# Batch 1's queries loaded ahead of the weights, softmax work spread over two slots, and a third output buffer, in a fused linear attention and highway layer

## The chip, the cores and the metric

The kernel runs on one core of a Trainium2 chip. The core has four compute engines that run beside each other, each through its own list of instructions in order: PE (matrix multiplies, into the accumulator memory PSUM), DVE (vector work), ACT (activations and copies) and POOL (vector work that can't reach PSUM). SP only starts transfers (DMAs) between main memory and on-chip memory. The metric is device time in microseconds (us), and the number compared is the median of repeated runs.

## The reference

The inputs are q, k and v of shape 8 x 8 x 576 x 64 (batch, head, sequence, head dimension), two weight matrices of 512 x 512 and a bias of 512. Attention without the square score matrix comes first: queries are softmaxed over the head dimension, keys over the sequence, and each head needs only a 64 x 64 product of keys and values. A highway layer follows.

```python
q_s = exp(q - max(q, -1));  q_s = q_s / (sum(q_s, -1) + 1e-09)
k_s = exp(k - max(k, 2));   k_s = k_s / (sum(k_s, 2) + 1e-09)
kv  = einsum('bhsd,bhse->bhde', k_s, v)
x   = einsum('bhsd,bhde->bhse', q_s, kv)      # then 4608 tokens x 512
H = maximum(x @ w_h, 0.0)
T = 1.0 / (1.0 + exp(-(x @ w_t + b_t)))
out = T * H + (1.0 - T) * x
```

## The kernel before

**Attention of one batch.** Each of the 8 batches has its q, k and v loaded as float32 tiles of 128 partitions x 2304, 1.18 MB each (`load`, L92). ACT takes the exponential of q and k in two halves each (`exp_half`, L154: 128 x 1152 to fp16). DVE sums the exponentials of q over the head dimension (`q_sums`, L199) and takes the reciprocal. The scaling of q by it has three forms: on DVE with an fp16 copy of the reciprocals (`q_scale_v`, L206 to L212, batches 0 and 2), by halves on POOL and DVE (`q_scale_half`, L217 to L227, batch 1), and on POOL (`q_scale_p`, L236, batches 3 to 7). PE transposes the scaled queries (`q_trans`, tile pq) and DVE copies them out (qsT, L253). POOL casts v to fp16 (`cast_v`, L161), PE multiplies keys and values (`kv_half`, tile psk), and DVE normalises the product (`kv_norm`, L186 and L188, tile kvn). PE multiplies queries by it (`x_pair` and `x_left`, tiles px and px_l). ACT copies three of the four px tiles into xT (L275), and DVE the fourth (L277) and the two small leftovers (L290, tile x9, which collects the last 64 rows of every batch).

**Highway layer of one batch.** The layer runs on transposed x, in four blocks of 128 output columns. `gate(c, ob)` is four matmuls (tile pt, 128 x 512) and a tanh on ACT (L308); `carry(c, ob)` is four matmuls (tile ph) and one DVE instruction for max(H, 0) - x (tile dd, L317); `blend(c, ob)` is one DVE instruction that multiplies the two (tile g, L325). `out_tile` turns x and g back by matmuls with identities (tile nat), copies them to an output buffer (ACT, L356, and in the last group also DVE, L354) and after every fourth tile starts a DMA of 1 MB (L359). Index c = 8 stands for the leftover rows; `most9` and `last9` write them.

**What sets the order.** Nothing is scheduled by a tool: each engine executes its instructions in the order in which the code emits them. A first list (L452 to L468) is emitted, then a table of events by half steps p. Slot c is the eight steps from p = 8c to 8c + 7, with the highway layer of batch c; the attention work of batch c + 1 is placed in the same slot, and part of the softmax of the next. Waits follow from data and from buffers. PSUM has eight banks: four for pt and ph in turn (`ps_ht`), three for pq, psk and px in turn (`ps_q`) and one for nat. Since the four `ps_ht` banks go round, gate or carry number n waits until DVE has finished with number n - 4.

**Transfers.** All loads and stores are started by SP in one order: q, k and v of batch 0 in halves, the bias, w_t, w_h, then q, k, v of batch 1, and so on; stores stand between the loads of later batches. The load tiles rotate over three buffers for each of q, k and v, and the weights use one turn of the q and the k tiles. The weights are cast to fp16 by DVE (w16t and one block of w16h) and POOL (three blocks of w16h). The output buffer o32 has two turns; the leftover rows have a buffer of their own (o9). In the last group, the second output buffer of group 3 is the one that group 2's second DMA reads.

Of the kernel before, what the change touches and what calls it, by code (L numbers as in the profile page):

```python
# [9 lines left out]
FP32 = mybir.dt.float32  # L10
FP16 = mybir.dt.float16
# [7 lines left out]
def kernel(  # L19
# [180 lines left out]

    NG = [(0, 4), (4, 8), (8, 9)]

    def q_scale_v(b):
        r32 = qsum[b]
        r2 = small.tile([P, 4 * N9, 2], FP16, tag="r2", name=f"r2_{b}")
        nc.vector.reciprocal(r32, r32)  # L206
        flat = r32.rearrange("p n c -> p (n c)")
        nc.vector.tensor_copy(r2, flat.broadcast_to([P, 4 * N9, 2]))
        e = eq[b].rearrange("p n c (w t) -> p (n c) w t", t=2)
        rb = r2.unsqueeze(2).broadcast_to([P, 4 * N9, 32, 2])  # L210
        for s in (slice(0, 16), slice(16, 4 * N9)):
            nc.vector.tensor_mul(e[:, s], e[:, s], rb[:, s])  # L212

    def q_scale_half(b, a, eng):
        h = slice(2 * a, 2 * a + 2)
        r32 = qsum[b][:, :, h]
        nc.vector.reciprocal(r32, r32)  # L217
        if eng is nc.gpsimd:
            e = eq[b][:, :, h, :]
            eng.tensor_mul(e, e, r32.broadcast_to(list(e.shape)))  # L220
            return
        r2 = small.tile([P, N9, 2, 2], FP16, tag="r2h", bufs=1, name=f"r2_{b}_{a}")
        nc.vector.tensor_copy(r2, r32.broadcast_to([P, N9, 2, 2]))
        e = eq[b][:, :, h, :].rearrange("p n c (w t) -> p n c w t", t=2)
        for c in range(2):
            rb = r2[:, :, c].unsqueeze(2).broadcast_to([P, N9, 32, 2])
            nc.vector.tensor_mul(e[:, :, c], e[:, :, c], rb)  # L227

    def q_recip(b):
        nc.vector.reciprocal(qsum[b], qsum[b])  # L230

    def q_scale_p(b, i):
        s = (slice(0, 4), slice(4, N9))[i]
        e = eq[b][:, s]
        r = qsum[b][:, s]
        nc.gpsimd.tensor_mul(e, e, r.broadcast_to(list(e.shape)))  # L236

    def q_trans(b, g, eng=None):
# [142 lines left out]
    def last9():  # L381
        t = ps_ht.tile([P, 4, P], FP32, tag="ht", name="nat9_l")
# [9 lines left out]
    def at(p, *fs):  # L392
        events.setdefault(p, []).extend(fs)

    E = lambda f, *a: (lambda: f(*a))

    for c in range(B + 1):
# [4 lines left out]
    for c in range(B + 1):  # L402
        for ob in range(4):
            at(8 * c + 2 * ob + 2, E(blend, c, ob))

# [7 lines left out]
                at(p + 1 + i // 2, E(out_tile, g, i, True))  # L413
    at(8 * B + 8, E(most9), E(last9))

    at(0, E(exp_half, 1, "q", 1))
    at(1, E(q_sums, 1, 0), E(q_scale_half, 1, 0, nc.gpsimd))
    at(3, E(q_sums, 1, 1), E(q_scale_half, 1, 1, nc.vector))
    at(5, E(exp_half, 1, "k", 0), E(cast_v, 1, 0))
    at(6, E(exp_half, 1, "k", 1), E(cast_v, 1, 1))  # L420
    at(7, E(q_trans, 1, 0), E(q_trans, 1, 1, nc.scalar), E(q_trans, 1, 2))
    at(7, E(kv_half, 1, 0), E(kv_half, 1, 1), E(kv_norm, 1))
    at(7, E(x_pair, 1, 0), E(x_pair, 1, 1), E(x_left, 1))
    for b in range(2, B):
        p = 8 * (b - 1)
        s = p + {2: 0, 3: -4}.get(b, -5)
        at(s, E(exp_half, b, "q", 0))
        at(s + 1, E(exp_half, b, "q", 1), E(q_sums, b, 0))
        at(s + 2, E(q_sums, b, 1))
        if b == 2:  # L430
            at(s + 2, E(q_scale_v, b))
        else:
            at(s + 2, E(q_recip, b), E(q_scale_p, b, 0))
            at(s + 3, E(q_scale_p, b, 1))
        s = p + {2: 2, 3: 0}.get(b, -1)
        at(s, E(exp_half, b, "k", 0), E(cast_v, b, 0))
# [12 lines left out]
    for b in range(2, B):  # L449
        at(8 * max(b - 3, 0), *[E(load, b, w) for w in "qkv"])  # L450

    for f in [  # L452
        E(warm_up, 20),
        E(exp_half, 0, "q", 0), E(q_sums, 0, 0),
        E(exp_half, 0, "q", 1), E(q_sums, 0, 1),
        E(q_scale_v, 0),
        E(exp_half, 0, "k", 0), E(cast_v, 0, 0),
        E(exp_half, 0, "k", 1), E(cast_v, 0, 1),
        E(q_trans, 0, 0), E(q_trans, 0, 1), E(warm_up, 2), E(q_trans, 0, 2),
        E(warm_up, 6),  # L460
        E(kv_half, 0, 0), E(gate_bias), E(warm_up, 2), E(kv_half, 0, 1), E(kv_norm, 0),
        E(warm_up, 4),
        E(x_pair, 0, 0), E(warm_up, 2), E(x_pair, 0, 1), E(warm_up, 2), E(x_left, 0),
        E(warm_up, 2),
        *[E(cast_weight, "t", k_, nc.vector) for k_ in range(4)],
        *[E(cast_weight, "h", k_, (nc.gpsimd, nc.vector)[k_ // 3]) for k_ in range(4)],
        E(exp_half, 1, "q", 0),
    ]:  # L468
        f()
    for p in range(8 * (B + 1) + 1):  # L470
        for f in events.pop(p, []):
            f()
    assert not events, events
# [30 lines left out]
```

## Time and profile before

| | |
|---|---|
| median of 13 runs | 148.41 us |
| lowest to highest | 146.84 to 151.21 us |
| the profiled execution's own time | 148.12 us |
| its span in the trace | 146.2 us |
| PE, DVE, ACT, POOL busy | 122.8, 108.2, 88.0, 43.9 us |

The difference between the profiled execution's time and its span, 1.9 us, lies around the span. The profile gives for each group of instructions the busy time, the mean duration and the idle time of the engine just before it, with what ended that idle time. The chain of waits is followed back from the last instruction to what released it. A view by windows gives the busy time of each engine in any stretch, with PEclk, the clock that TensorE was granted (1.00 is full speed), and what the DMA engines moved. A timeline lists instructions in order of time with the idle time in front of them. Several instructions on one timeline row overlap a little, so the distance between starts is what one costs its engine.

### The profile page before, as it was taken

The numbers are of one execution on the slowest core, as the hardware profiler recorded it, in microseconds if no ns is written. First come the engines' busy times: TensorE is split into PE (matmuls) and PEld (weight loads), VectorE is DVE, ScalarE is ACT, GpSimd is POOL, SyncE is SP. The second block draws the span as 40 slices with busy tenths as digits, with TensorE's granted clock in tenths as the row PEclk, the third lists the DMA queues.
The fourth block names the chain that finished last, engine by engine and source line by source line (L and its number), as shares of the span: only waits on it lengthen the run. The fifth ranks groups of instructions, "written<-read, shape, count | busy, mean of one in ns | idle before, by whom it ended". The sixth has DMA issues, their size and how long they took to land.

```text
span 146.2 us, 3509 instructions
## 1 busy us (share of the span) xinstructions
PE 122.8 (84%) x1465; PEld 66.6 (46%) x1465; DVE 108.2 (74%) x201; ACT 88.0 (60%) x125; POOL 43.9 (30%) x38
## 2 busy tenths in 40 slices
PE   4979968355908968997999899899989999999940
PEld 1345323143405422663664475466447555577530
DVE  1493579993698696699679988987998666574860
ACT  3660409724683546769869778796973664552630
POOL 2006042901400019605920890393098000000000
PEclk9999999999996895999999999999999999999997
DMA  4999999999999999500399999993006006037466
GB/s 161 345 400 390 401 404 411 411 412 415 402 410 411 412 404 412 206 2 0 135 276 409 404 313 364 402 395 119 0 4 287 9 0 287 0 141 318 191 263 239
DMA packets 16023, 40.06 MB, mean 274 GB/s; under 512 B 644, under 2 KB 1672, under 8 KB 14984
## 3 DMA queue, kind: packets, MB, share of 16 engines
q1 hardware_dynamic: 16008, 39.85, 71.1%
q8 instruction: 11, 0.18, 0.5%
q14 instruction: 4, 0.03, 0.1%
HBM read 30.41 MB, written 9.44 MB: 273 GB/s over the span
## 4 chain that ended last, share of the span: by engine, by line
PE 50%; DVE 33%; DMA 7%; ACT 4%; issue 2%; SPq 0%; DVEq 0%; ACTq 0%
PE pt L59 15%; PE ph L59 14%; DVE r L199 11%; PE nat L59 6%; PE pq L64 5%; DVE g L325 5%; DVE dd L317 5%; PE psk L59 5%; DMA out_dram<-o 4%; DMA q<-in_q_dram 3%; PE warm L59 3%; PE px L59 2%; DVE xT L277 2%; ACT eq L154 2%; DVE w16t L111 1%
## 5 line engine op out<-in xcount | busy, mean ns | idle before, releaser
L308 ACT ACTIVATE pt<-pt,bt 128x512 f32<-128x512 f32 x36 | 23.8, 663 | 27.4 <-PE pt L59 27.4
L59 PE MATMUL pt<-xT,w16t 128*128 128x512 f16 x128 | 35.5, 393 | 3.7 <-DVE xT L277 2.6
L59 PE MATMUL ph<-xT,w16h 128*128 128x512 f16 x128 | 34.3, 392 | 3.7 <-DVE g L325 3.7
L236 POOL TENSOR_TENSOR eq<-eq,r 128x1024 f16<-128x1024 f16 (+1 forms) x10 | 21.0, 2117 | 42.5 <-DVE r L230 42.5
L317 DVE SCALAR_TENSOR_TENSOR dd<-ph,xT 128x512 f16<-128x512 f32 x32 | 21.9, 686 | 10.8 <-PE ph L59 10.8
L325 DVE SCALAR_TENSOR_TENSOR g<-pt,dd 128x512 f16<-128x512 f32 x36 | 24.4, 678 | 1.4
L199 DVE TENSOR_REDUCE r<-eq 128x18 f32<-128x1152 f16 x16 | 21.5, 1345 | 4.0 <-ACT eq L154 3.9
L161 POOL CAST v<-v 128x1152 f16<-128x1152 f32 x16 | 18.2, 1162 | 17.0 <-DMA v<-in_v_dram 10.1
L154 ACT ACTIVATE eq<-q 128x1152 f16<-128x1152 f32 x16 | 18.4, 1163 | 6.7 <-DMA q<-in_q_dram 6.7
L59 PEld LDWEIGHTS <-w16h 128*128 128x128 f16 x144 | 12.7, 100 | 18.1 <-issue 8.5
L59 PEld LDWEIGHTS <-w16t 128*128 128x128 f16 x144 | 12.8, 99 | 16.1 <-DVE w16t L111 2.5
L154 ACT ACTIVATE ek<-k 128x1152 f16<-128x1152 f32 x16 | 18.5, 1169 | 1.6 <-DMA k<-in_k_dram 1.6
L59 PE MATMUL nat<-half_i,g 128*128 128x128 f16 x140 | 18.9, 219 | 0.2 <-DVE g L325 0.2
L356 ACT COPY o<-nat 128x512 f32<-128x512 f32 x28 | 16.5, 591 | 3.4 <-PE nat L59 2.8
L275 ACT CAST xT<-px 128x512 f16<-128x512 f32 x24 | 13.4, 592 | 8.2 <-PE px L59 8.0
L59 PE MATMUL nat<-ident,xT 128*128 128x128 f16 x128 | 17.3, 219 | 0.0
L64 PE MATMUL pq<-ident,eq 128*128 128x128 f16 x144 | 12.1, 224 | 4.7 <-DVE eq L212 4.7
L59 PEld LDWEIGHTS <-g 128*128 128x128 f16 x144 | 14.0, 98 | 4.1 <-DVE g L325 0.6
L253 DVE COPY qsT<-pq 128x1024 f16<-128x1024 f16 (+1 forms) x23 | 12.4, 548 | 4.3 <-PE pq L64 4.2
L59 PEld LDWEIGHTS <-xT 128*128 128x128 f16 x128 | 12.5, 98 | 5.2 <-issue 2.4
L59 PE MATMUL warm<-wide,ident 128*128 128x512 f16 x40 | 12.8, 464 | 1.9 <-DVE wide L140 1.9
L64 PEld LDWEIGHTS <-eq 128*128 128x128 f16 x144 | 9.7, 100 | 8.3 <-ACT ek L154 5.6
(48 smaller groups left out, 88.7 us busy)
## 6 DMA issues: line engine op xcount, KB each, us to landing
out_dram<-o SPq DMA_DIRECT2D x8, 1024.0 KB, 4.7
q<-in_q_dram SPq DMA_DIRECT2D x7, 1152.0 KB, 14.4
k<-in_k_dram SPq DMA_DIRECT2D x7, 1152.0 KB, 14.5
v<-in_v_dram SPq DMA_DIRECT2D x6, 1152.0 KB, 14.6
v<-in_v_dram SPq DMA_DIRECT2D x4, 576.0 KB, 11.0
q<-in_q_dram SPq DMA_DIRECT2D x2, 576.0 KB, 4.1
k<-in_k_dram SPq DMA_DIRECT2D x2, 576.0 KB, 7.1
w32t<-in_moe_w_t_dram SPq DMA_DIRECT2D x1, 1024.0 KB, 11.1
```

The lines of the kernel that those rows point to most:

```text
L59: mm = lambda o, l, r, st, sp: nc.tensor.matmul(o, l, r, start=st, stop=sp, skip_group_check=True)
L64: nc.tensor.matmul(o, i, ident, is_transpose=True, start=True, stop=True, skip_group_check=True,)
L154: nc.scalar.activation(dst[b][:, :, 2 * a : 2 * a + 2, :], in32[which][b][:, 2 * a : 2 * a + 2].rearrange("p c n d -> p n c d"), AF.Exp,)
L161: (eng or nc.gpsimd).tensor_copy(v16s[b % 2][:, :, 2 * a : 2 * a + 2, 0:64], in32["v"][b][:, 2 * a : 2 * a + 2].rearrange("p c n d -> p n ...
L199: nc.vector.reduce_sum(qsum[b][:, :, h], eq[b][:, :, h, :], axis=AX.X)
L236: nc.gpsimd.tensor_mul(e, e, r.broadcast_to(list(e.shape)))
L253: nc.vector.tensor_copy(qsT[b][:, :, n0:n1, :], t[:, :, 0:w, :])
L275: nc.scalar.copy(dst, t[c])
L308: nc.scalar.activation(ps, ps, AF.Tanh, bias=bt2[:, ob : ob + 1], scale=0.5)
L317: nc.vector.scalar_tensor_tensor(dd, ps, 0.0, xv(ob), op0=ALU.max, op1=ALU.subtract)
L325: nc.vector.scalar_tensor_tensor(gv(ob), th, 1.0, dd, op0=ALU.add, op1=ALU.mult)
L356: nc.scalar.copy(o, flat(t))
```

## The change

- The load of batch 1's queries is put ahead of the two weights on SP. Nothing else changes place on that queue.
- Slot 0 is no longer built from the table: its instructions are written out in the first list. Batch 1's exponentials stand on ACT directly behind batch 0's last copies, and its sums and scaling stand on DVE on both sides of the cast of w_t and ahead of all of slot 0's dd and g. It is scaled on DVE only. Two blocks of w16h are cast by ACT and two by POOL, none by DVE. Twelve more warm-up matmuls (tile warm) stand ahead of the first gate. Gates 0 and 1 stand ahead of carries 0 and 1, and batch 1's transposes and products stand between the later gates and carries.
- Batch 2's query exponentials and its first sum move from slot 1 to the end of slot 0. Its scaling moves from DVE to POOL (`q_scale_p`), the second half of its v cast moves from POOL to DVE, and its two products of keys and values stand one step earlier, its transposes one or no step later.
- Batch 3's query exponentials and sums move from the middle of slot 1 to its last two steps and the first step of slot 2; its scaling follows in slot 2, behind both of its v casts. Batch 4's query softmax moves from p = 19 to 22 to p = 20 to 23, and batch 4 takes the plan that batch 3 had.
- `q_scale_v` works on row groups 0 to 3 and 4 to 8 with an fp16 copy of the reciprocals for each, which is one small cast more (batches 0 and 1); `q_scale_half` is gone.
- The pool `og` has three buffers instead of two, and the leftover rows' buffer o9 becomes one turn of it.

On DVE in slot 0, from the weight cast on, before. The names are the tiles of the sections above with their shapes; r_1 are batch 1's sums, eq batch 1's queries, pt_0 and ph_0 the first block of batch 0's highway layer.

```order
L111 CAST w16t<-w32t 128x512 x4
L111 CAST w16h<-w32h 128x512
L317 SCALAR_TENSOR_TENSOR dd_0_369<-ph_0_364,xT_299 128x512
L199 TENSOR_REDUCE r_1_371<-eq_342 128x9x2
L217 RECIPROCAL r_1_371<-r_1_371 128x9x2
L325 SCALAR_TENSOR_TENSOR g_344<-pt_0_345,dd_0_369 128x8x64
L317 SCALAR_TENSOR_TENSOR dd_1_387<-ph_1_382,xT_299 128x512
L199 TENSOR_REDUCE r_1_371<-eq_342 128x9x2
L217 RECIPROCAL r_1_371<-r_1_371 128x9x2
L223 CAST r_1_1_391<-r_1_371 128x36
L227 TENSOR_TENSOR eq_342<-eq_342,r_1_1_391 128x9x64 x2
L325 SCALAR_TENSOR_TENSOR g_344<-pt_1_375,dd_1_387 128x8x64
```

The same place now.

```order
L199 TENSOR_REDUCE r_1_350<-eq_347 128x9x2
L111 CAST w16t<-w32t 128x512 x4
L199 TENSOR_REDUCE r_1_350<-eq_347 128x9x2
L204 RECIPROCAL r_1_350<-r_1_350 128x36
L210 CAST r_1_0_358<-r_1_350 128x32
L212 TENSOR_TENSOR eq_347<-eq_347,r_1_0_358 128x1024
L210 CAST r_1_4_361<-r_1_350 128x40
L212 TENSOR_TENSOR eq_347<-eq_347,r_1_4_361 128x1280
L297 SCALAR_TENSOR_TENSOR dd_0_389<-ph_0_384,xT_300 128x512
L305 SCALAR_TENSOR_TENSOR g_368<-pt_0_369,dd_0_389 128x8x64
```

Both sums and the whole scaling of batch 1 have moved in front of the first dd and g, and the w16h cast has left DVE.

On DVE at the end of slot 1 and the start of slot 2, before: kvn is batch 2's normalised product, r_3 are batch 3's sums, px_1_1 is batch 2's fourth product (it goes into xT), and g_344 with pt_2 and pt_3 are the last two blocks of slot 1.

```order
L188 TENSOR_TENSOR kvn_103<-psk_1_639,rz_725 128x128
L199 TENSOR_REDUCE r_3_731<-eq_676 128x9x2
L325 SCALAR_TENSOR_TENSOR g_344<-pt_2_621,dd_2_683 128x8x64
L199 TENSOR_REDUCE r_3_731<-eq_676 128x9x2
L230 RECIPROCAL r_3_731<-r_3_731 128x36
L317 SCALAR_TENSOR_TENSOR dd_3_757<-ph_3_752,xT_299 128x512
L277 CAST xT_740<-px_1_1_760 128x8x64
L290 CAST x_107<-px_l_767 128x2x64
L290 CAST x_107<-px_l_773 128x2x64
L325 SCALAR_TENSOR_TENSOR g_344<-pt_3_733,dd_3_757 128x8x64
```

The same place now.

```order
L188 TENSOR_TENSOR kvn_103<-psk_1_622,rz_713 128x128
L297 SCALAR_TENSOR_TENSOR dd_2_723<-ph_2_718,xT_300 128x512
L233 COPY qsT_666<-pq_1_725 128x4x256
L233 COPY qsT_666<-pq_2_735 128x4x64
L305 SCALAR_TENSOR_TENSOR g_368<-pt_2_659,dd_2_723 128x8x64
L297 SCALAR_TENSOR_TENSOR dd_3_762<-ph_3_757,xT_300 128x512
L257 CAST xT_746<-px_1_1_765 128x8x64
L270 CAST x_107<-px_l_772 128x2x64
L270 CAST x_107<-px_l_778 128x2x64
L199 TENSOR_REDUCE r_3_785<-eq_755 128x9x2
L305 SCALAR_TENSOR_TENSOR g_368<-pt_3_739,dd_3_762 128x8x64
L199 TENSOR_REDUCE r_3_785<-eq_755 128x9x2
```

Batch 3's sums stood in front of the cast of px_1_1 and now stand behind it.

The core of the diff:

```diff
-    og = pool("og", 2)
+    og = pool("og", 3)
...
     nc.sync.dma_start(brow, moe_b_t.rearrange("(k p) -> k p", p=P))
+    load(1, "q")
     load_weight("t", moe_w_t, "q32")
     load_weight("h", moe_w_h, "k32")
-    load(1, "q")
...
+    def q_scale_v(b, n0, n1):
+        w = 4 * (n1 - n0)
+        r2 = small.tile([P, w, 2], FP16, tag=f"r2_{w}", name=f"r2_{b}_{n0}")
+        r = qsum[b][:, n0:n1].rearrange("p n c -> p (n c)")
+        nc.vector.tensor_copy(r2, r.broadcast_to([P, w, 2]))
+        e = eq[b][:, n0:n1].rearrange("p n c (w t) -> p (n c) w t", t=2)
+        nc.vector.tensor_mul(e, e, r2.unsqueeze(2).broadcast_to([P, w, 32, 2]))
...
+        o9 = o32["last"] = og.tile([P, 4, 512], FP32, tag="o32", name="o9")
...
+    at(8, E(q_sums, 2, 1), E(q_recip, 2), E(cast_v, 2, 0), E(q_scale_p, 2, 0, 4))
+    at(9, E(exp_half, 2, "k", 0), E(q_scale_p, 2, 4, N9))
+    at(10, E(exp_half, 2, "k", 1))
+    at(11, E(cast_v, 2, 1, nc.vector))
...
+            s = p + {3: -2, 4: -4}.get(b, -5)
...
+            2: ((4, 5, 5), (3, 4), (6, 7, 7)),
+            3: ((4, 5, 5), (3, 4), (6, 7, 7)),
+            4: ((2, 3, 4), (4, 5), (6, 6, 7)),
...
-        E(warm_up, 2),
+        E(warm_up, 14),
+        E(exp_half, 1, "q", 0), E(exp_half, 1, "q", 1),
+        E(q_sums, 1, 0),
         *[E(cast_weight, "t", k_, nc.vector) for k_ in range(4)],
-        *[E(cast_weight, "h", k_, (nc.gpsimd, nc.vector)[k_ // 3]) for k_ in range(4)],
-        E(exp_half, 1, "q", 0),
+        E(q_sums, 1, 1), E(q_recip, 1), E(q_scale_v, 1, 0, 4), E(q_scale_v, 1, 4, N9),
+        *[E(cast_weight, "h", k_, (nc.gpsimd, nc.scalar)[k_ % 2]) for k_ in range(4)],
+        E(gate, 0, 0), E(gate, 0, 1), E(exp_half, 1, "k", 0), E(cast_v, 1, 0),
+        E(carry, 0, 0), E(blend, 0, 0), E(carry, 0, 1), E(blend, 0, 1),
+        E(exp_half, 1, "k", 1), E(cast_v, 1, 1),
+        E(q_trans, 1, 0), E(q_trans, 1, 1), E(q_trans, 1, 2),
+        E(gate, 0, 2), E(carry, 0, 2), E(blend, 0, 2),
+        E(kv_half, 1, 0), E(gate, 0, 3), E(kv_half, 1, 1), E(kv_norm, 1),
+        E(carry, 0, 3), *[E(load, b, w) for b in (2, 3) for w in "qkv"],
+        E(exp_half, 2, "q", 0),
+        E(x_pair, 1, 0), E(x_pair, 1, 1), E(blend, 0, 3), E(x_left, 1),
+        E(exp_half, 2, "q", 1), E(q_sums, 2, 0),
```

More of the change, by code (lines that the diff above doesn't have):

```diff
@@ L201, with q_scale_p @@
     NG = [(0, 4), (4, 8), (8, 9)]
[L203 to L227, printed above, removed]
     def q_recip(b):
         nc.vector.reciprocal(qsum[b], qsum[b])
[L232 to L235, printed above, removed]
+    def q_scale_v(b, n0, n1):
[5 more added lines that the diff above has]
+        nc.vector.tensor_mul(e, e, r2.unsqueeze(2).broadcast_to([P, w, 32, 2]))
+    def q_scale_p(b, n0, n1):
+        e, r = eq[b][:, n0:n1], qsum[b][:, n0:n1]
         nc.gpsimd.tensor_mul(e, e, r.broadcast_to(list(e.shape)))
@@ L381, in last9 @@
     def last9():
+        o9 = o32["last"]
         t = ps_ht.tile([P, 4, P], FP32, tag="ht", name="nat9_l")
@@ L395 @@
     E = lambda f, *a: (lambda: f(*a))
-    for c in range(B + 1):
+    for c in range(1, B + 1):
         for ob in range(4):
@@ L401 @@
             at(p + 1, E(carry, c, ob))
-    for c in range(B + 1):
+    for c in range(1, B + 1):
         for ob in range(4):
@@ L448 @@
         at(p + x[2], E(x_left, b))
-    for b in range(2, B):
-        at(8 * max(b - 3, 0), *[E(load, b, w) for w in "qkv"])
+    for b in range(4, B):
+        at(8 * (b - 3), *[E(load, b, w) for w in "qkv"])
     for f in [
@@ L455 @@
         E(exp_half, 0, "q", 1), E(q_sums, 0, 1),
-        E(q_scale_v, 0),
+        E(q_recip, 0), E(q_scale_v, 0, 0, 4), E(q_scale_v, 0, 4, N9),
         E(exp_half, 0, "k", 0), E(cast_v, 0, 0),
@@ L463 @@
         E(x_pair, 0, 0), E(warm_up, 2), E(x_pair, 0, 1), E(warm_up, 2), E(x_left, 0),
-        E(warm_up, 2),
+        E(warm_up, 14),
+        E(exp_half, 1, "q", 0), E(exp_half, 1, "q", 1),
+        E(q_sums, 1, 0),
         *[E(cast_weight, "t", k_, nc.vector) for k_ in range(4)],
-        *[E(cast_weight, "h", k_, (nc.gpsimd, nc.vector)[k_ // 3]) for k_ in range(4)],
-        E(exp_half, 1, "q", 0),
+        E(q_sums, 1, 1), E(q_recip, 1), E(q_scale_v, 1, 0, 4), E(q_scale_v, 1, 4, N9),
[10 more added lines that the diff above has]
+        E(exp_half, 2, "q", 1), E(q_sums, 2, 0),
     ]:
         f()
-    for p in range(8 * (B + 1) + 1):
+    for p in range(8, 8 * (B + 1) + 1):
         for f in events.pop(p, []):
```

35 lines of the change are left out of this document (12 added, 23 removed).

## The prediction

> **What bounds the kernel now.** I read the windows first, to find stretches with different limits, then PE's timeline where PE idles, then DVE's timeline and the chain of waits for what PE waits for. The windows (PE, PEld, DVE, ACT, POOL busy, granted clock, DMA share, GB/s):
>
> ```profile
> 25.00:30.00 5.00, 1.89 (x8) 0.78 (x8) 4.90 (x8) 3.31 (x4) 4.11 (x3) 1.00 1.04 411
> 40.00:45.00 5.00, 1.05 (x11) 0.57 (x10) 4.90 (x8) 3.34 (x4) 0.00 (x0) 1.00 1.04 409
> 90.00:100.00 10.00, 9.56 (x119) 5.45 (x119) 9.23 (x15) 8.58 (x13) 6.37 (x4) 1.00 0.97 388
> ```
>
> Late slots are full on PE with DVE close behind. In slots 0 and 1, PE is busy 1.89 and 1.05 of 5 us while DVE is busy 4.90. So time can be won in the first slots, by having DVE do first what PE waits for. PE's timeline there:
>
> ```profile
> 30.07 1.02 PE L59 MATMUL ph<-xT,w16h 128*128 128x512 f16 x4 [3.17 <-DVE g L325]
> 36.79 1.04 PE L59 MATMUL pt<-xT,w16t 128*128 128x512 f16 x4
> 44.36 0.61 PE L64 MATMUL pq<-ident,eq 128*128 128x128 f16 x8 [3.95 <-DVE eq L212]
> 55.45 0.59 PE L59 MATMUL pt<-xT,w16t 128*128 128x512 f16 x1 [1.27 <-DVE xT L277]
> 68.85 1.04 PE L59 MATMUL pt<-xT,w16t 128*128 128x512 f16 x4
> ```
>
> Slot 1 begins at 36.79, slot 2's first gate gets its last matmul at 55.45, slot 3 begins at 68.85. PE waits 3.17 us for a PSUM bank that DVE's g frees, 3.95 us for batch 2's scaled queries, 1.27 us for a cast. DVE was busy with sums and scaling in each case. Slot 3's first gate, four matmuls that start 0.22 apart, gets its last one near 69.5.
>
> **The change, part by part.** I follow DVE's new list from 17.7 us on with the distances between its rows, and cross to PE or ACT where the list has to wait. Prices, first from the chain of waits, where instructions run back to back:
>
> ```profile
> 8.87 0.21 DVE r L208
> 9.11 0.70 DVE eq L212
> ...
> 32.01 0.61 DVE qsT L253
> ...
> 64.23 0.41 PE psk L59 x36
> ...
> 69.89 0.45 PE nat L59 x8
> 70.34 0.86 PE ph L59 x4
> ...
> 76.68 0.23 DVE rz L186 x2
> 76.91 0.46 DVE kvn L188 x2
> 77.36 1.26 DVE r L199
> 78.62 0.60 DVE dd L317
> ```
>
> Timeline rows, and from the view of one tile the least, median and longest of the w16t casts in ns:
>
> ```profile
> 17.71 0.49 DVE L290 CAST x<-px_l 128x128 f16<-128x128 f32 x2
> 18.12 2.51 DVE L111 CAST w16t<-w32t 128x512 f16<-128x512 f32 x4
> 42.88 0.38 DVE L206 RECIPROCAL r<-r 128x36 f32<-128x36 f32 x1
> 21.57 1.16 ACT L154 ACTIVATE eq<-q 128x1152 f16<-128x1152 f32 x1 [4.00 <-DMA q<-in_q_dram]
> 34.89 1.66 ACT L275 CAST xT<-px 128x512 f16<-128x512 f32 x3 [1.85 <-PE px L59]
> 54.43 4.19 POOL L236 TENSOR_TENSOR eq<-eq,r 128x1024 f16<-128x1024 f16 x2 [16.20 <-DVE r L230]
> L111 DVE CAST w16t<-w32t x4: 409/754/827, 18.1 to 20.2; 128x512 f16<-128x512 f32 x4
> ```
>
> So a sum is 1.3 us, dd, g, qsT and DVE's xT cast 0.6 each (qsT's third part 0.2), normalising 0.7, a reciprocal 0.4, DVE's scaling 0.2 + 0.7 for each of two parts, a gate or carry 0.9 on PE, a half of the key and value product 0.4, as much for a pair of px.
>
> *Slot 0.* The bytes ahead of k of batch 1 stay the same, so w_h lands when q of batch 1 landed before, 21.6, and batch 1's q the two weights earlier, ahead of ACT being free. The one small cast more in batch 0 pushes its second transpose by 0.2. With it, the small copies end at 18.4 and ACT has the first exponential at 18.95. DVE: sum 20.3, w16t 22.8, sum 24.1, reciprocal and two scalings 26.3, dd, g, dd, g 28.7, three qsT 30.1. Meanwhile ACT's two w16h casts and gates 0 and 1 fit in, and PE's carry 0 (from 23.7) waits for nothing. The first g is thus later than before. But batch 1 is then ready: PE does one product (0.4), gate 3 (0.9) and the other product by 31.6, normalising ends at 32.3, px follows. ACT has gate 3's tanh and batch 2's first exponential (1.2) until 33.1, then three xT casts to 34.8; slot 1 begins at 35.0 against 36.79: **1.8 us gained**. The fourteen warm matmuls (3.0 from about 18) end before w16t is complete at 22.8 and cost nothing. The weights' later landing is covered by DVE's own work: dd of block 0 waits for DVE until 26.3, while ph is done near 24.6; without that cover it would cost up to the 2.9 us by which q goes ahead (1.18 MB at 410 GB/s). Behind ACT's two waiting casts stand only tanh 0 and 1, whose gates end later.
>
> *Slot 1.* xT, g and the copies take DVE to 35.7; two sums and reciprocal, 38.6; dd, g, dd, 40.4; the v cast that moved here, which no row shows at 1152 columns: between 0.9 (2.25 times the 0.41 of the shortest cast of 512) and 1.9 (the same from the longest, 0.83, beside POOL's casts); I take 1.4, the middle, since POOL scales at that time. Then g, qsT, normalising, dd, qsT: 44.9. PE does px (0.4) and carry 3 (0.9) to 46.2 and px again. ACT has batch 3's exponential between its second and third xT cast, so the third ends at 48.35, the leftovers follow, and slot 2's first gate gets its last matmul at 49.2 against 55.45: **6.3 gained in all**. Batch 2's scaling on POOL runs from 38.6 to 42.8; its second transposes need a PSUM bank that normalising frees at 43.5, so POOL is covered by 0.7; batch 3's v casts behind it have until 53.
>
> On this the Trainium skill speaks against the change: GPSIMD Engine Reference, section 4.1 Engine selection, puts elementwise work on VectorE, since GpSimd is about twice as slow with two inputs. The rows agree in kind: 4.19 against some 1.4 for the two scalings. By that rule batch 2's scaling would stay on DVE; by the rows that makes DVE's list, the later one here, 1.8 longer and the sum below 144.2 instead of 142.4.
>
> *Slot 2* carries batch 3's two sums and batch 4's. DVE: copies 48.8, sum 50.1, g 50.7, sum and reciprocal 52.4, dd, g, dd, g 54.8. PE then does gate 2, an output tile (0.45) and the first transposes to 55.4; qsT 56.0, normalising 56.7, dd 57.3, qsT 58.1, sum, g, sum and reciprocal 61.7, dd, xT 62.9. Slot 3's first gate gets its last matmul at 62.9 against 69.5, and DVE's list stands 6.4 earlier after it: **6.4 gained in all** is what I carry on. POOL's scaling (52.4 to 56.6) again just meets the transposes.
>
> *Slots 3 to 8.* The usual distance between slots, and when batch 2's v lands:
>
> ```profile
> 82.08 0.38 PE L59 MATMUL pt<-xT,w16t 128*128 128x512 f16 x1 [0.43 <-DVE xT L277]
> ...
> 94.65 0.38 PE L59 MATMUL pt<-xT,w16t 128*128 128x512 f16 x1 [0.43 <-DVE xT L277]
> 35.99 2.24 POOL L161 CAST v<-v 128x1152 f16<-128x1152 f32 x2 [6.88 <-PE px L59]
> ```
>
> A slot takes 12.6. Batch 4 now has the plan that batch 3 had in slot 2, which took 14.0 (55.45 to 69.5) with 1.7 lost to a half clock (below), so 12.3: nothing is won or lost there. DMA can't take the gain back: POOL gets batch 2's v at 36.0 and PE's product of it comes at 38.2, one cast later; the loads behind it are needed 12.6 apart and land 8.6 apart (3.5 MB at 410 GB/s).
>
> *The tail.* These rows are from the chain and from ACT's, PE's and DVE's timelines:
>
> ```profile
> 129.49 5.75 DMA out_dram<-o
> 135.34 0.59 ACT L356 COPY o<-nat 128x512 f32<-128x512 f32 x1 [2.81 <-PE nat L59]
> 137.29 1.03 PE L59 MATMUL ph<-x,w16h 128*128 128x512 f16 x4
> 139.44 0.69 DVE L325 SCALAR_TENSOR_TENSOR g<-pt,dd 128x512 f16<-128x512 f32 x1
> ```
>
> ACT's copy waits 2.81 us; it is put down to PE, but the chain shows the store of 5.75 us that holds the buffer. A third buffer removes that. Late next is PE: its last carry ends at 138.3 either way. Then dd and g end at 138.9 and 139.5 where g now ends at 139.44 + 0.69 = 140.1, so about **0.5** is gained, not 2.8 (bounds 0.2 to 0.9: the last stores also come closer together). The leftover rows' buffer waits for the store that lands at 135.2, before its first write.
>
> *The sum.* The profiled execution took 148.1; less 6.4 and 0.5 gives 141.2. One cost is open, the clock. PE's busy time and granted clock in three windows of 3.4 us:
>
> ```profile
> 28.30:31.70 3.40, 1.62 (x18) 1.00 1.04 412
> 52.10:55.50 3.40, 1.64 (x17) 0.99 1.04 410
> 55.50:58.90 3.40, 3.40 (x9) 0.50 1.04 412
> ```
>
> After the window with 1.64 busy, the next 3.4 us ran at half clock, which costs PE 1.7; after the one with 1.62 they did not, so the limit lies about there. In my walk PE is busy some 1.6 of 3.4 us around 46 and 1.4 around 61; the first is followed by a stretch that DVE sets. Between 0 and two windows (3.4 us) I take half of one, 0.9: 142.1. The profiled execution lies 0.3 below the median of 148.4, so I forecast **142.4**.
>
> [...]
>
> **Rivals.**
> - *No half clock at all.* My walk has no PE gap above 2.5 us after 26; if only long gaps count, the 0.9 falls away: 141.5. For it: a gap of 3.17 us that did no harm. Against: the half clock after 1.27. [...] Chance 0.15.
> - *POOL sets batches 2 and 3.* The cover is 0.7 and about nothing. If POOL slows beside DVE's casts by a third, its 4.2 become 5.5 and PE's transposes wait 0.7 in slot 1 and 1.3 in slot 2: 144.4. Against: its 4.19 stands beside a busy DVE already. Chance 0.12.
> - *Only slot 0's gain stays.* Slots 1 and 2 take as long as before because the work in them is the same: 148.4 - 1.8 - 0.5 = 146.1. For it: PE's half clock made slot 2 long, and could again. Against: the 3.95 and 1.27 waits have work in front of them now. Chance 0.12.
> - *The half clock returns over and over: slower.* Slots 0 to 2 have many short gaps in the new order. If every second window from 28 to 63 us falls below about 1.64 busy, five windows run at half clock, and 5 x 1.7 = 8.5 on 141.5 is 150.0. With four it is 148.3, no change; from five on it is slower. For it: my walk is within a few tenths of the limit at two places. Against: DVE sets much of that stretch and would hide part. Chance 0.12, of which 0.07 slower and 0.05 the same.
>
> **How the numbers follow.** My forecast has 0.49. Faster: 0.49 + 0.15 + 0.12 + 0.12 = 0.88. Runs of this kernel can't tell less than about 0.5%, 0.7 us, from no change; same 0.05, slower 0.07. The range leaves out the last rival (0.12) and a little at the fast end: low 139.8 is 1.7 below 141.5, of which the bounds of the v cast give 0.5 and of the tail 0.4, and the rest my rounding up by 0.04 (1.26 to 1.3) of some twenty instructions; high 146.4, just over the third rival.
>
> **What would show it.** Right: slot 1's first gate near 35, slot 2's complete near 49.5, slot 3's near 63, then 12.6 per slot; DVE without idle time over 0.8 us from 35 to 63; no 2.8 us wait of ACT near the end. Wrong: PE waiting for POOL's eq, half clock in more than two windows after 28 us, or slot 1 or 2 longer than 14.5 us.

## The result, and the profile after

| | before | after |
|---|---|---|
| median | 149.09 us (48 runs) | 141.40 us (11 runs) |
| ratio, with its 95% interval | | 0.9539 (0.9507 to 0.9570) |
| the profiled execution's own time | 148.12 us | 141.43 us |
| its span | 146.2 us | 139.2 us |

The kernel is 4.6% faster; 142.4 was forecast, with 139.8 to 146.4 as the range. Medians are over all runs of a comparison, while ratios leave out runs that were disturbed, so a ratio isn't quite the quotient of two medians. Line numbers have moved: in the changed kernel dd is L297, g L305, qsT L233, DVE's xT cast L257, the scaling L212 on DVE and L216 on POOL.

From the page of the changed kernel come the totals, the clock by 40 slices, and the share of the chain of waits by engine:

```profile
span 139.2 us, 3531 instructions
PE 122.3 (88%) x1477; PEld 66.3 (48%) x1477; DVE 106.4 (76%) x200; ACT 88.0 (63%) x126; POOL 44.4 (32%) x37
PEclk9999999999999999999999999999999999999997
PE 50%; DVE 29%; ACT 5%; POOL 5%; DMA 3%; issue 3%; SPq 0%; DVEq 0%; POOLq 0%
```

The busy times are nearly those of before (PE 122.8, DVE 108.2): work wasn't removed, idle time was. The clock row is at 90% or more in every slice but the last, where PE is done. POOL is 5% of the chain. The three windows of the prediction, now (PE, PEld, DVE, ACT, POOL busy, granted clock, DMA share, GB/s):

```profile
25.00:30.00 5.00, 3.59 (x58) 2.04 (x58) 4.68 (x10) 1.98 (x3) 2.30 (x2) 1.00 1.04 411
40.00:45.00 5.00, 4.20 (x68) 2.35 (x69) 4.62 (x11) 0.84 (x2) 3.03 (x3) 1.00 1.04 405
90.00:100.00 10.00, 9.57 (x152) 5.41 (x150) 8.89 (x17) 8.08 (x12) 3.80 (x4) 1.00 0.25 99
```

PE is busy 3.59 and 4.20 of 5 us where it was busy 1.89 and 1.05, and the late slots are as full as before. PE's timeline at the marks that the prediction named:

```profile
34.20 1.04 PE L59 MATMUL pt<-xT,w16t 128*128 128x512 f16 x4
40.14 0.62 PE L64 MATMUL pq<-ident,eq 128*128 128x128 f16 x8 [0.49 <-POOL eq L216]
42.87 0.73 PE L64 MATMUL pq<-ident,eq 128*128 128x128 f16 x10 [0.61 <-POOL eq L216]
47.34 1.04 PE L59 MATMUL pt<-xT,w16t 128*128 128x512 f16 x4
61.92 0.38 PE L59 MATMUL pt<-xT,w16t 128*128 128x512 f16 x1 [0.85 <-DVE xT L257]
74.10 1.04 PE L59 MATMUL pt<-xT,w16t 128*128 128x512 f16 x4
87.33 0.38 PE L59 MATMUL pt<-xT,w16t 128*128 128x512 f16 x1 [0.43 <-DVE xT L257]
```

The waits of 3.17 and 3.95 us are gone; in their place stand two short ones, 0.49 and 0.61, for POOL's scaling. With four matmuls 0.22 apart, the last matmul of slot 2's first gate starts at 48.0 and that of slot 4 at 74.76. DVE's timeline:

```profile
20.05 1.42 DVE L111 CAST w16t<-w32t 128x512 f16<-128x512 f32 x4
24.96 0.69 DVE L297 SCALAR_TENSOR_TENSOR dd<-ph,xT 128x512 f16<-128x512 f32 x1
33.41 0.69 DVE L257 CAST xT<-px 128x512 f16<-128x512 f32 x1 [0.77 <-PE px L59]
39.88 0.88 DVE L161 CAST v<-v 128x1152 f16<-128x1152 f32 x1
45.81 0.69 DVE L297 SCALAR_TENSOR_TENSOR dd<-ph,xT 128x512 f16<-128x512 f32 x1 [0.80 <-PE ph L59]
```

The four weight casts take 1.42 us where they took 2.51. The longest idle times of DVE up to 62 us, once batch 1's sums have begun, are the 0.77 and 0.80 shown here. POOL's scaling of batches 2 and 3, two instructions each:

```profile
38.18 4.63 POOL L216 TENSOR_TENSOR eq<-eq,r 128x1024 f16<-128x1024 f16 x2 [1.33 <-DVE r L204]
51.41 4.19 POOL L216 TENSOR_TENSOR eq<-eq,r 128x1024 f16<-128x1024 f16 x2 [4.38 <-DVE r L204]
```

The end of the changed kernel, from the timelines of ACT, DVE and SP:

```profile
126.29 0.59 ACT L336 COPY o<-nat 128x512 f32<-128x512 f32 x1 [1.07 <-issue]
133.59 0.42 DVE L367 COPY o<-nat_l 128x256 f32<-128x256 f32 x1
134.04 0.41 SPq L368 DMA_DIRECT2D out_dram<-o  x1
```

And the same two last rows of before:

```profile
141.19 0.42 DVE L386 COPY o<-nat_l 128x256 f32<-128x256 f32 x1
141.65 0.41 SPq L387 DMA_DIRECT2D out_dram<-o  x1
```

So the lead over before can be followed: 36.79 - 34.20 = 2.6 us at slot 1, 55.45 - 48.0 = 7.4 at slot 2, 69.5 - 61.9 = 7.6 at slot 3, 82.08 - 74.76 = 7.3 at slot 4, 94.65 - 87.33 = 7.3 at slot 5, 141.19 - 133.59 = 7.6 at the last copy, and 146.2 - 139.2 = 7.0 at the end of the span: the last store needs 139.2 - 134.04 = 5.16 us where it needed 146.2 - 141.65 = 4.55.

### The profile page after: what moved, and what is told of

Read it like the earlier page. It is cut to its first block, busy times and chain, and to the rows that moved or that the text cites. A ratio compares the mean times of both kernels' runs of the same rounds, so it can differ in the third digit from the quotient of the medians.

```text
span 139.2 us, 3531 instructions
## 1 busy us (share of the span) xinstructions
PE 122.3 (88%) x1477; PEld 66.3 (48%) x1477; DVE 106.4 (76%) x200; ACT 88.0 (63%) x126; POOL 44.4 (32%) x37
## 4 chain that ended last, share of the span: by engine, by line
PE 50%; DVE 29%; ACT 5%; POOL 5%; DMA 3%; issue 3%; SPq 0%; DVEq 0%; POOLq 0%
PE pt L59 14%; PE ph L59 13%; DVE r L199 12%; PE nat L59 8%; POOL eq L216 5%; PE pq L64 4%; DVE g L305 4%; PE psk L59 3%; DMA q<-in_q_dram 3%; DVE dd L297 3%; PE warm L59 3%; ACT eq L154 2%; DVE eq L212 2%; PE px L59 2%; DVE r L204 2%
## 5 line engine op out<-in xcount | busy, mean ns | idle before, releaser
L59 PE MATMUL pt<-xT,w16t 128*128 128x512 f16 x128 | 33.3, 380 | 2.2 <-DVE xT L257 1.7
L216 POOL TENSOR_TENSOR eq<-eq,r 128x1024 f16<-128x1024 f16 (+1 forms) x12 | 25.6, 2153 | 29.9 <-DVE r L204 29.9
L59 PE MATMUL ph<-xT,w16h 128*128 128x512 f16 x128 | 32.8, 380 | 0.0
L297 DVE SCALAR_TENSOR_TENSOR dd<-ph,xT 128x512 f16<-128x512 f32 x32 | 21.8, 682 | 7.6 <-PE ph L59 7.5
L305 DVE SCALAR_TENSOR_TENSOR g<-pt,dd 128x512 f16<-128x512 f32 x36 | 24.5, 682 | 1.8
L161 POOL CAST v<-v 128x1152 f16<-128x1152 f32 x15 | 16.9, 1148 | 22.7 <-DMA v<-in_v_dram 22.7
L59 PEld LDWEIGHTS <-w16h 128*128 128x128 f16 x144 | 12.3, 98 | 11.8 <-issue 1.4
L59 PE MATMUL warm<-wide,ident 128*128 128x512 f16 x52 | 15.4, 445 | 1.9 <-DVE wide L140 1.9
L233 DVE COPY qsT<-pq 128x1024 f16<-128x1024 f16 (+1 forms) x24 | 12.8, 553 | 3.2 <-PE pq L64 3.0
L59 PEld LDWEIGHTS <-xT 128*128 128x128 f16 x128 | 12.5, 98 | 5.5 <-issue 2.6
L64 PE MATMUL pq<-ident,eq 128*128 128x128 f16 x144 | 11.5, 219 | 2.4 <-POOL eq L216 1.4
L64 PEld LDWEIGHTS <-eq 128*128 128x128 f16 x144 | 8.9, 98 | 6.3 <-POOL eq L216 3.1
## 6 DMA issues: line engine op xcount, KB each, us to landing
q<-in_q_dram SPq DMA_DIRECT2D x7, 1152.0 KB, 13.7
```

Source lines behind the costliest of these rows:

```text
L59: mm = lambda o, l, r, st, sp: nc.tensor.matmul(o, l, r, start=st, stop=sp, skip_group_check=True)
L64: nc.tensor.matmul(o, i, ident, is_transpose=True, start=True, stop=True, skip_group_check=True,)
L161: (eng or nc.gpsimd).tensor_copy(v16s[b % 2][:, :, 2 * a : 2 * a + 2, 0:64], in32["v"][b][:, 2 * a : 2 * a + 2].rearrange("p c n d -> p n ...
L233: nc.vector.tensor_copy(qsT[b][:, :, n0:n1, :], t[:, :, 0:w, :])
L297: nc.vector.scalar_tensor_tensor(dd, ps, 0.0, xv(ob), op0=ALU.max, op1=ALU.subtract)
L305: nc.vector.scalar_tensor_tensor(gv(ob), th, 1.0, dd, op0=ALU.add, op1=ALU.mult)
```

## The experiments

My theory: DVE's list sets slots 0 to 2, and its new order gives nearly all; the earlier load of batch 1's queries pays only together with the new list of slot 0. The rivals tried against it: the third output buffer gives a part of it; the gain is mostly the half clock that went; POOL sets slot 1; the twelve warm-up matmuls are needed.

**The third buffer, by itself in the kernel before.**

```diff
-    og = pool("og", 2)
+    og = pool("og", 3)
...
-    o9 = consts.tile([P, 4, 512], FP32, name="o9")
...
+        o9 = o32["last"] = og.tile([P, 4, 512], FP32, tag="o32", name="o9")
```

> The kernel before with nothing but the third output buffer and the leftover rows' buffer as one turn of it. The prediction's theory gives it 0.5 us (148.6 against 149.1). A rival, from the trace of the changed kernel, where the arithmetic ended 0.3 earlier than the front explains and the last stores ran slower: it brings nothing that can be measured (149.0 to 149.3). If the wait of 2.8 us were all won, 146.3.

149.28 us against 149.37; ratio 0.9949 (0.9899 to 0.9999). That leaves room for anything from nothing to 1.5 us.

**The changed kernel with two output buffers and the leftover rows' own.** The same lines the other way round.

> The changed kernel with two output buffers and a leftover buffer of its own, as before. The prediction's theory: 0.5 slower, 141.9. The rival that the buffer brings nothing: 141.4. If the third buffer carries the gain in the tail, 144.2.

141.32 us; ratio to before 0.9470 (0.9428 to 0.9512): no slower than with three. The wait of ACT's copy is there. From its timelines, this copy and DVE's last one, and from its chain of waits, the last carry:

```profile
128.10 0.58 ACT L336 COPY o<-nat 128x512 f32<-128x512 f32 x1 [2.36 <-PE pt L59]
134.10 0.42 DVE L366 COPY o<-nat_l 128x256 f32<-128x256 f32 x1
```

```profile
130.65 0.88 PE ph L59 x4
```

The last carry in the changed kernel's chain:

```profile
130.14 0.88 PE ph L59 x4
```

From the carry to the last copy it is 134.10 - 130.65 = 3.45 us with the wait of 2.36, and 133.59 - 130.14 = 3.45 without it. The wait ran beside PE's list and cost nothing.

**Only slot 0 new: batches 2 to 4 on the plan of before.**

```diff
-    at(8, E(q_sums, 2, 1), E(q_recip, 2), E(cast_v, 2, 0), E(q_scale_p, 2, 0, 4))
...
+        s = p + {2: 0, 3: -4}.get(b, -5)
...
+        if b == 2:
+            at(s + 2, E(q_scale_v, b, 0, 4), E(q_scale_v, b, 4, N9))
...
-        E(exp_half, 2, "q", 0),
...
-        E(exp_half, 2, "q", 1), E(q_sums, 2, 0),
```

> The changed kernel with its slot 0 and load order, but batches 2, 3 and 4 on the plan of the kernel before in slots 1 and 2 (batch 2 scaled on DVE in slot 1, batch 3's sums ahead of the cast that slot 2 waits for). The prediction's theory says that the order in slots 1 and 2 brings the larger part: only the 2.6 of slot 0 stay, 146.0 to 146.5. The rival that the better part of the gain is the clock (no half clock once slot 0 is dense): 143 to 144.5. PE's half clock should come back in slot 1 by the first theory.

145.92 us; ratio 0.9739 (0.9678 to 0.9800), in the same comparison in which the run above had 0.9470. So the new order of slots 1 and 2 is worth 0.9739 - 0.9470 = 2.7%, 4.0 us. PE's wait for batch 2 is back, and the half clock behind it (PE busy, granted clock, DMA share, GB/s), so the 4.0 us hold what that costs here. The profiled execution took 148.41 us, well over the median, so no times between slots are read from it:

```profile
45.72 1.01 PE L64 MATMUL pq<-ident,eq 128*128 128x128 f16 x8 [3.93 <-DVE r L210]
```

```profile
45.70:49.10 3.40, 3.38 (x20) 0.50 1.04 412
```

**The kernel before, with PE kept busy.** Matmuls into the nat bank whose result nobody reads, in the two gaps that came ahead of the half clock.

```diff
+    at(11, E(warm_nat, 16))
...
+    at(15, E(warm_nat, 6))
```

> The kernel before with 16 warm-up matmuls in PE's wait of 3.95 us in slot 1 and 6 ahead of slot 2's first gate, so that no window of 3.4 us is short of PE work; nothing else is changed. It prices the half clock by itself. If the order on DVE's list is what counts, DVE sets most of these stretches and 1 to 1.7 us go: 147.4 to 148.1. If the half clock is most of the gain, 3.4 or more: 145.7 or less. If only gaps above 3 us brought it, the second six matmuls do nothing, and 1.7 at most goes.

147.50 us against 149.37; ratio 0.9865 (0.9810 to 0.9921), 2.0 us less. Two windows at 45.1 and 55.5 us, where the clock was 0.54 and 0.50 before (PE busy, granted clock, DMA share, GB/s), and in PE's timeline the first gates of slots 2 and 3:

```profile
45.10:48.80 3.70, 3.70 (x64) 1.00 1.04 409
55.50:58.90 3.40, 3.40 (x29) 1.00 1.04 412
```

```profile
54.47 1.16 PE L59 MATMUL pt<-xT,w16t 128*128 128x512 f16 x4
66.98 1.04 PE L59 MATMUL pt<-xT,w16t 128*128 128x512 f16 x4
```

Without the half clock slot 2 of before takes 66.98 - 54.47 = 12.5 us. The half clock in these two stretches thus cost before about 2 us. In the profiled execution of before they are the only two while PE works, and 3.4 us at half clock take at most 1.7 us of work from PE, so they hold at most 3.4 of the 7.6 us won up to slot 3: the smaller part there. Over all executions its share is less certain. In this execution two other half-clock stretches came, from 30.9 and 37.7 us on. And among the runs that the ratios use the mean granted clock was 0.946 to 0.972 in the kernel before (0.970 in the profiled execution, so near the top) and 0.985 to 0.995 in the changed kernel. A straight line through the 37 such runs of the kernel before gives 0.5 us for 0.01 of clock; from their mean of 0.958 to the changed kernel's 0.990 that is an estimate of 1.7 us, which reaches beyond the clocks that were measured.

**The weights loaded first, in the changed kernel.**

```diff
-    load(1, "q")
     load_weight("t", moe_w_t, "q32")
     load_weight("h", moe_w_h, "k32")
+    load(1, "q")
```

> The changed kernel with batch 1's queries loaded behind the two weights, as before. The first theory: DVE's list in slot 0 begins with batch 1's sum, which then waits for the exponential until some 22.8 instead of 18.8, so slot 1 starts 3 to 4 us later and the time is 144.4 to 145.4. Rival: batch 1's v lands at 27 either way and its products set slot 1, so only 1 to 2 us are lost: 142.4 to 143.4. If the load order does not matter, 141.4.

146.50 us against 148.79; ratio 0.9858 (0.9817 to 0.9899): 5.1 us more than the changed kernel, more than I had expected. DVE waits for batch 1's exponentials, and since its weight casts stand behind them in its list, PE waits too and falls to half clock:

```profile
22.76 1.35 DVE L199 TENSOR_REDUCE r<-eq 128x18 f32<-128x1152 f16 x1 [4.36 <-ACT eq L154]
```

```profile
24.50 3.60 PE L59 MATMUL pt<-xT,w16t 128*128 128x512 f16 x8 [3.30 <-DVE w16t L111]
39.08 1.04 PE L59 MATMUL pt<-xT,w16t 128*128 128x512 f16 x4
```

Slot 1 begins at 39.08 instead of 34.20, 4.9 us later, and that stays to the end.

**Batch 1's queries loaded first, in the kernel before.** The same three lines, the other way round.

> The kernel before with nothing changed but batch 1's queries loaded ahead of the two weights. The prediction holds that the weights' later landing (2.9 us) is only free because DVE's list was rewritten to work on batch 1 meanwhile; in the old list the first gates wait for the weights, so 1 to 2.9 slower: 150 to 152. Rival: the load order is worth its gain by itself, since batch 1's exponentials start 4 us earlier: 146 to 148.

152.11 us against 149.52; ratio 1.0214 (1.0118 to 1.0311): slower by 3.2 us. Nothing covers the later weights; PE waits for w16h, and DVE for PE, and slot 1 begins at 40.22 instead of 36.79:

```profile
22.22 2.15 PE L59 MATMUL ph<-xT,w16h 128*128 128x512 f16 x4 [2.36 <-POOL w16h L111]
40.22 1.04 PE L59 MATMUL pt<-xT,w16t 128*128 128x512 f16 x4
```

```profile
24.49 0.69 DVE L317 SCALAR_TENSOR_TENSOR dd<-ph,xT 128x512 f16<-128x512 f32 x1 [2.80 <-PE ph L59]
```

Part of the 3.2 us is the clock: this execution has four stretches at half clock, the profiled one of before two. With the run above this makes a pair: the new load order costs 3.2 us with the old list, and the old load order costs 5.1 with the new list. In slot 0 neither half is a gain by itself, since slot 1 begins at 40.22 and 39.08, both later than the 36.79 of before. The kernel with the new list and the old load order is as a whole still 2.1 us faster than before (ratio 0.9858), as it has the new order of slots 1 and 2.

**Batch 2 scaled on DVE, in the changed kernel.**

```diff
-    at(8, E(q_sums, 2, 1), E(q_recip, 2), E(cast_v, 2, 0), E(q_scale_p, 2, 0, 4))
-    at(9, E(exp_half, 2, "k", 0), E(q_scale_p, 2, 4, N9))
+    at(8, E(q_sums, 2, 1), E(q_recip, 2), E(cast_v, 2, 0), E(q_scale_v, 2, 0, 4))
+    at(9, E(exp_half, 2, "k", 0), E(q_scale_v, 2, 4, N9))
```

> The changed kernel with batch 2 scaled on DVE (two small casts and two multiplies, 1.8 us) instead of POOL. The prediction's theory: DVE's list is the later one in slot 1, so 0.5 to 1.8 slower, 141.9 to 143.2. Rival, from the trace of the changed kernel: there POOL's scaling of 4.6 us ends last in slot 1 (it is on the chain of waits), so without it 0.5 to 1 us is won: 140.4 to 140.9.

142.13 us; ratio 0.9560 (0.9521 to 0.9599): 0.7 us more than the changed kernel's 141.40. PE's two waits for POOL go, and longer ones for DVE come:

```profile
39.78 1.02 PE L59 MATMUL pt<-xT,w16t 128*128 128x512 f16 x4 [1.39 <-DVE dd L297]
42.66 0.48 PE L59 MATMUL psk<-v,ek 64*64 64x65 f16 x36 [1.41 <-DVE v L161]
48.58 1.04 PE L59 MATMUL pt<-xT,w16t 128*128 128x512 f16 x4
```

POOL is on the chain, yet taking its work away makes slot 2's first gate 48.58 - 47.34 = 1.2 later: DVE is the scarcer engine there. The last matmul of slot 3's first gate is 1.25 later too (63.17 against 61.92); the last store then takes 4.81 us to the end instead of 5.16, which is most of the difference to the 0.7 of the medians.

**Two warm-up matmuls instead of fourteen.**

```diff
-        E(warm_up, 14),
+        E(warm_up, 2),
```

> The changed kernel with 2 warm-up matmuls ahead of the first gate instead of 14, so that PE idles some 2.7 us from 18.3. If a window of 3.4 us with less than 1.64 of PE work brings the half clock, the first gates and carries take 3.6 us instead of 1.9 each pair, DVE's dd and g wait for them, and the time is 142.4 to 144. If only gaps above 3 us bring it, 141.4.

141.47 us; ratio 0.9522 (0.9482 to 0.9562): the same as the changed kernel. PE does get a half clock (PE busy, granted clock, DMA share, GB/s), after a gap of 2.00 us:

```profile
18.20:21.60 3.40, 1.40 (x6) 1.00 1.05 409
21.60:25.20 3.60, 3.60 (x10) 0.54 1.04 411
```

```profile
20.48 2.98 PE L59 MATMUL pt<-xT,w16t 128*128 128x512 f16 x8 [2.00 <-DVE w16t L111]
34.44 1.04 PE L59 MATMUL pt<-xT,w16t 128*128 128x512 f16 x4
```

But slot 1 begins at 34.44, 0.2 later only: DVE has its sums and scalings to do meanwhile. The extra warm-ups keep the clock up and buy no time.

**DVE's gaps filled.** If DVE's list sets slots 1 and 2, a sum that moves from behind what PE waits for into an idle stretch of DVE should show in the time. First batch 2's first sum, into the 0.77 us ahead of the xT cast at 33.41:

```diff
-        E(x_pair, 1, 0), E(x_pair, 1, 1), E(blend, 0, 3), E(x_left, 1),
-        E(exp_half, 2, "q", 1), E(q_sums, 2, 0),
+        E(x_pair, 1, 0), E(q_sums, 2, 0), E(x_pair, 1, 1), E(blend, 0, 3), E(x_left, 1),
+        E(exp_half, 2, "q", 1),
```

> The changed kernel with one instruction moved: batch 2's first sum (1.3 us on DVE) stands ahead of the cast of batch 1's last product, in a gap of 0.8 us in which DVE waits for PE. If DVE's list is what sets slot 1, 0.5 to 0.8 is won: 140.6 to 140.9. If POOL's scaling or PE sets it, the same, 141.4; if slot 1's first gate, which now waits 0.5 longer for the cast, sets it, 141.9.

Then, on top of that, batch 3's as well, into the 0.80 us at 45:

```diff
+            if b == 3:
+                at(12, E(exp_half, 3, "q", 0))
+                at(13, E(exp_half, 3, "q", 1))
+                at(14, E(q_sums, 3, 0))
+                at(16, E(q_sums, 3, 1), E(q_recip, 3))
```

> As the run with batch 2's first sum earlier, and also batch 3's two exponentials in ACT's idle time of 4.2 us in slot 1 and its first sum ahead of DVE's last dd of slot 1, where DVE waits 0.8. If DVE's list sets slots 1 and 2, together 1.2 to 2 us are won: 139.4 to 140.2. If POOL or PE sets slot 2, what the other run gives, or 0.3 less.

140.54 us, ratio 0.9478 (0.9419 to 0.9537), and 139.44 us, ratio 0.9425 (0.9353 to 0.9496); both in one comparison, against 149.52. That is 0.9 and 2.0 us below the changed kernel's 141.40, which was timed in another comparison. It is a little more than the gaps of 0.77 and 0.80 hold, and where the rest comes from wasn't isolated. In the second, the sums stand where DVE idled, and slot 2's first gate comes earlier:

```profile
32.59 1.34 DVE L199 TENSOR_REDUCE r<-eq 128x18 f32<-128x1152 f16 x1
44.10 1.34 DVE L199 TENSOR_REDUCE r<-eq 128x18 f32<-128x1152 f16 x1
```

```profile
46.16 1.04 PE L59 MATMUL pt<-xT,w16t 128*128 128x512 f16 x4
60.13 0.38 PE L59 MATMUL pt<-xT,w16t 128*128 128x512 f16 x1 [1.00 <-DVE xT L257]
```

47.34 - 46.16 = 1.2 us at slot 2, and 61.92 - 60.13 = 1.8 at slot 3. This shows that the place of the sums sets the time, but not that DVE alone does: POOL's scaling of batch 2 waits for these sums and starts earlier with them, at 37.42 and 37.35 in the two runs instead of 38.18. The expectation that the time would stay the same if POOL set slot 1 had overlooked that. What speaks for DVE there is the run with batch 2 scaled on DVE.

**The better version with two output buffers.** Once with the leftover rows' buffer of their own, as in the kernel before, and once with it as a turn of the pool.

```diff
-    og = pool("og", 3)
+    og = pool("og", 2)
```

> The kernel with the earlier sums of batches 2 and 3, and with two output buffers and a leftover buffer of its own. If the third buffer brings nothing, 139.4. If it brings 0.3 by earlier copies and the stores behind the last copy give 0.5 back (5.1 us from the last store's issue to the end of the span in the traces with it, 4.6 without), 139.2. By the prediction's 0.5: 139.9.

> The same with two output buffers, but the leftover rows' buffer as one turn of them. If the place of the leftover buffer is what makes the last stores slower, 5.1 us again from the last store's issue to the end and 139.4 or up to 0.3 above; if the number of buffers does (earlier stores of group 3 that lie closer to the last ones), 4.6 and 139.2.

139.82 us, ratio 0.9357 (0.9297 to 0.9417), and 139.72 us, ratio 0.9393 (0.9325 to 0.9461), both against 149.27, beside 139.44 with three. Nothing that can be measured. The last store is issued at 132.36 in a span of 137.2 in the first, and at 132.24 in a span of 137.4 in the second:

```profile
132.36 0.41 SPq L367 DMA_DIRECT2D out_dram<-o  x1
```

```profile
132.24 0.41 SPq L368 DMA_DIRECT2D out_dram<-o  x1
```

That is 4.84 and 5.16 us to the end. Three turns and a buffer of its own would tell number and place apart the other way; it wasn't tried.

## Why the prediction was right, point by point

It was right in direction and cause, and the time came within 1.0 us of the forecast; some of that is luck, since several terms were off by up to 0.9 us and cancelled. Against its own profiled execution the prediction had 6.4 from the slots, 0.5 from the tail and 0.9 lost to the clock: 148.1 to 142.1. Measured were 7.3 from the slots, 0.3 lost at the end (7.0 of span), no half clock, and 0.3 more around the span (141.43 - 139.2 = 2.2 us, where it was 1.9): 7.3 - 0.3 - 0.3 = 6.7, from 148.12 to 141.43.

- *Slot 0: 1.8 forecast, 2.6 measured.* The term that was mis-sized is the cast of w_t: 2.5 us taken over from the row of before, 1.42 measured. There the casts ran beside POOL's casts of w_h (17.91 to 20.02). Now w_h lands later, POOL casts it from 21.3, when three of the four casts of w_t are done, and each takes 0.42, about the least of the 409/754/827 that the prediction quotes. They take 0.42 also in the run with batch 1's queries first in the kernel before, which has the old list and the later w_h. So the edit that moves a load also changed the price of an instruction, and the walk had missed that. That the later weights cost nothing, because DVE gets to the first dd later than PE gets to the first ph, held: dd starts at 24.96 without idle time. That this cover is needed was shown from both sides (the new load order alone is 3.2 slower than before, the new list without it 5.1 slower than the changed kernel).
- *Slot 1: 6.3 in all forecast, 7.4 measured.* Of the 1.2 us by which slot 2's first gate is ahead of the forecast (49.2 to 48.0), 0.8 came from slot 0. The v cast took 0.88, the lower bound, where 1.4 was taken. Against it stands POOL: its scaling took 4.63 instead of 4.19, and the cover of 0.7 was gone. PE waited 0.49 and 0.61, which the prediction had named as a mark of being wrong: POOL is on the chain. A part of the rival "POOL sets batches 2 and 3" thus came in slot 1, and less in slot 2, where POOL took 4.19 and PE waited 0.29 for it. Why it took 4.63 was not isolated; DVE's v cast stands beside the slower one.
- *The sentence on where elementwise work belongs.* By the rule of the Trainium skill (GPSIMD Engine Reference, section 4.1 Engine selection), that elementwise work on a tile goes to VectorE, batch 2 would have stayed there, and the prediction put that at 1.8 us. Measured was 0.7. The sign held; the walk had left out that PE's waits for POOL, 0.49 and 0.61, would go. That these alone account for the difference isn't shown: in the trace slots 2 and 3 come 1.2 later, and the rest lies in the last store. The rule is right that POOL is the slower engine, by about three times here where it says about two (4.63 us against 0.69 + 0.82 for the two multiplies on DVE in slot 0), and didn't decide, since DVE had no room.
- *Slot 2: 6.4 in all forecast, 7.6 measured*, by what slot 1 brought; the slot itself took 13.9 where 13.7 was forecast (62.9 - 49.2).
- *Slots 3 to 8: nothing forecast.* Slot 3 took 74.76 - 61.92 = 12.8 where 12.3 was forecast for the plan that batch 4 took over, so 0.3 of the lead went there; after it the lead stayed at 7.3. That batch 3's slot before would take 12.3 without its half clock was about right: 12.5 with PE kept busy.
- *The tail: 0.5 forecast, nothing measured.* This step failed. That ACT's wait of 2.81 would go and PE's last carry be late next was right: the wait is gone. But what was booked as the gain of the third buffer came with two buffers just as well (3.45 us from carry to last copy in both), and 0.6 was given back by the last store. So the third buffer brings nothing that can be measured.
- *The clock: 0.9 set aside, none came* in the profiled execution. The walk put PE's busy time at 1.6 of 3.4 us near 46 and at 1.4 near 61; PE was busier than that. The emptiest stretches of 3.4 us in the changed kernel (PE busy, granted clock, DMA share, GB/s) are these:

```profile
25.75:29.15 3.40, 2.08 (x16) 1.00 1.04 412
58.90:62.30 3.40, 2.13 (x20) 1.00 0.39 153
```

 So the rival without half clock, at 141.5, had the better time, but its condition, that only long gaps count, is not borne out by the other runs. The Trainium skill (TensorE: Matmul & The Clock Gate, section Why this matters for your kernels) advises against PE gaps above about 3 us; the changed kernel has no such gap and no half clock, in keeping with that, but the run with two warm-ups has the half clock after a gap of 2.00 us, with 1.40 of 3.4 us busy, and the run with batch 1's queries first in the kernel before has one after 2.36 (four matmuls took 2.15 us there instead of 1.03). The prediction's limit near 1.64 of 3.4 us busy is not borne out either. In the kernel before with PE kept busy the half clock came after 2.00 of 3.4 us busy, with no gap above 0.66:

```profile
34.25:37.65 3.40, 2.00 (x19) 1.00 1.04 409
37.65:41.05 3.40, 3.40 (x10) 0.51 1.04 409
```

 In the kernel before with batch 1's queries first the clock stayed at 1.00 after 1.55 of 3.4 us busy (42.30 to 45.70 us). Neither a gap nor this busy share alone sorts these cases, and the 2.08 of the changed kernel lie only just above the 2.00.
- *Only slot 0's gain* (146.1) would have been the time without the new order of slots 1 and 2: that kernel took 145.9. It failed as a rival because what that order brings was real, 4.0 us with the half clock that it avoids. *Half clock over and over* did not come, as PE was never less busy than 2.08 of 3.4 us.

What stays open: why POOL's scaling of batch 2 is 0.4 us slower than that of batch 3, what makes the last store longer, how much of the gain over all executions is the half clock that went, and what brings the half clock.

## What to carry to other kernels

Read the stage in which the busiest engine is full and the matrix engine is empty, and write down that engine's list in order: what nobody waits for yet can go into its idle stretches, and what others wait for can go forward into them (0.9 and 2.0 us here from moving sums into one and two gaps of 0.8). Here an earlier load was worth something only because the engine that waits for the load pushed back got other work to do first; undo each half by itself to see that. A wait at the end that runs beside the matrix engine's own list, like the one for an output buffer here, can be worth nothing that is measurable even if it is 2.8 us long.

## What the runs showed of the hardware that was not expected

- The cast of 128 x 512 from float32 to fp16 on DVE took 0.42 us when POOL hardly cast beside it, and up to 0.83 in the kernel before, where POOL did. The run with batch 1's queries first in the kernel before, where POOL's casts come later, has 0.42 too (0.419 to 0.427). So the price of this cast depends on whether POOL casts beside it.
- From the issue of the last store to the end of the span it took 4.55, 4.84, 4.51, 4.52 and 4.84 us in the five profiled executions in which the leftover rows have a buffer of their own (before, and the runs with two buffers, with PE kept busy, with batch 1's queries first, and the better version with two buffers), and 5.12 to 5.25 in most of those in which their buffer is a turn of the pool (5.16 in the changed kernel; 4.81 with batch 2 scaled on DVE and 4.85 with the third buffer alone are the exceptions). The number of turns makes no difference: 5.15 with three and 5.16 with two in the better version. The cause is open.
- A half clock of some 3.5 us needn't cost anything: 0.2 us at slot 1 in the run with two warm-ups, where DVE sets the pace, while two such stretches cost about 2.0 us in the kernel before.
- The half clock came after 3.4 us in which PE was busy 2.00 us and never idle longer than 0.66 us at a time (the kernel before with PE kept busy).
